# Attention with QK norm, then a mixture of experts: gathers for experts 1 to 4 in a row, and the last expert's second layer with its 16 last tokens first

## The chip, the cores and the metric

The kernel runs on one core of a Trainium2 chip. The metric is the device time of one execution in microseconds (us); lower is better. Three runs of the kernel before took 411.0, 411.21 and 412.35 us, so its median is 411.21 us.

## What is computed

The reference has two parts. The first is attention over 8 batches of 12 heads of 448 tokens with 64 numbers each, with queries and keys normalised (root mean square). The second is a mixture of experts on the 3,584 rows of 768 numbers that this gives: a gate chooses one of 8 experts for each row, each expert keeps the 80 rows with the largest gate weights, and the rest of the output is zero.

```
logits = x @ w_gate
expert_idx = np.argmax(logits, axis=1)
...
out = np.zeros((N, D), dtype=np.float32)
for e in range(E):
    ...
    if len(tok_idx) > capacity:
        gw = gate_w[tok_idx]
        keep = np.argpartition(-gw, capacity)[:capacity]
        tok_idx = tok_idx[keep]
    h = np.maximum(x[tok_idx] @ w1[e], 0.0)
    out[tok_idx] = gate_w[tok_idx, None] * (h @ w2[e])
```

Here E is 8, the capacity 80, w1[e] is 768 x 1024 and w2[e] 1024 x 768.

## The kernel before

The attention takes most of the time. It is followed by a short stage that ends the choice of rows: while earlier batches run, a list of the best 80 rows of each expert is carried along, and after the last batch the lists are made final. The chosen row numbers are written by VectorE into idxG (80 rows by 8 experts, L1115). Attention rows lie in a DRAM tensor, xr_scratch, 780 numbers a row (768 and 12 factors that normalise its heads).

Then comes the expert loop (L1252). Experts are counted from 0 here, as in the code, so "expert 1" is the second one. Expert 0 takes its tokens from matmuls in the stage before. For experts 1 to 7 a gather (L1139), an indirect DMA that GpSimd issues, brings the 80 rows xg into SBUF; VectorE multiplies each by its factors into xn (normal, L1190, three pieces of 256 columns, L1194); TensorE transposes xn (xpose, L1199, pxt, L1209), and a copy puts the result into xgT.

For each expert TensorE does the first layer (ph, L1260: 8 chunks of 128 hidden columns in two halves), and ScalarE takes each half through ReLU into h_sb (L1267). The transposes of the next expert's tokens stand behind the first layer, and behind them the second layer. That has two parts. main (L1239) does the first 64 tokens: 16 matmuls of 384 columns into py, whose upper and lower 64 partitions are the two halves of the output columns. rest (L1245) does the last 16 tokens: 32 matmuls into pz, four quarters on 32 partitions each. rest is done for experts 0 and 7 alone, and for the others in pairs (1 and 2, 3 and 4, 5 and 6) after the second of the pair. VectorE multiplies py by the gate weights into yo (L1284) and pz into yr (L1296), and GpSimd scatters each to the output rows (scatter, L1221, the DMA of L1223).

The order on each engine is the order of the code. GpSimd issues gathers and scatters one after the other on one queue. gather has two ways to hold a transfer back: wait=True puts a memset on VectorE ahead of it, behind=... a copy of one column out of a tile of TensorE's, here the first half of ph of expert 0:

```
            if e == fh == 0:
                gather(2, ph[:CAP, 0, 0:1])
                gather(3)
```

Weights of experts 6 and 7 come late, on SyncE's queue, into the tiles of experts 0 and 1. held (L1229), called behind the first piece of xn of expert 1, starts the first of them; fetch_late (L253) the next two; the last, the second-layer weights of expert 7, are two DMAs of six and two of the eight chunks (L1310), issued after the pair of experts 1 and 2 is done.

Of the kernel before, what the change touches and what calls it, by code (L numbers as in the profile page):

```python
# [10 lines left out]
F32 = mybir.dt.float32  # L11
BF16 = mybir.dt.bfloat16
AF = mybir.ActivationFunctionType
ALU = mybir.AluOpType
# [7 lines left out]
def kernel(  # L22
# [13 lines left out]
    nc = tc.nc  # L36
# [3 lines left out]
    E = moe_w_gate.shape[1]  # L40
    F = moe_w1.shape[2]
    CAP = int(moe_capacity)
# [903 lines left out]
    mpool = mlate[0]  # L946
# [73 lines left out]
    for j in range(NT):  # L1020
        nc.scalar.activation(tied[:, j], row[:, j * 128:(j + 1) * 128], AF.Identity,
                             scale=-1.0, bias=gw[:, j:j + 1])
# [11 lines left out]
    for h in range(4):  # L1034
# [3 lines left out]
                             scale=xo[:, DM + h:DM + h + 1])  # L1038
# [9 lines left out]
    for j in range(NT):  # L1048
# [9 lines left out]
                            op0=ALU.add, op1=ALU.is_lt)  # L1058
# [63 lines left out]
            chosen(1, False)  # L1122
    outs = dram_disjoint_views(out, E + E // 2 + 1)
    xgs = {}
    def gather(e, behind=None, wait=False):

        if e == 1:
            xgs[e] = tpool.tile([128, 1024], F32, tag="beat", name="xg")[:CAP, :XW]
        elif e % 4 == 3:
            xgs[e] = prep.tile([128, NJ + 1, 256], F32, tag="xb", name="xg")[  # L1130
                :CAP].rearrange("p j d -> p (j d)")[:, :XW]
        else:
            xgs[e] = upool.tile([128, 2, S], F32, tag="us", name="xg")[:CAP].rearrange(
                "p u s -> p (u s)")[:, :XW]
        if wait:
            nc.vector.memset(xgs[e][:, 0:1], 0.0)
        if behind is not None:
            nc.vector.tensor_copy(xgs[e][:, 0:1], behind)
        nc.gpsimd.indirect_dma_start(  # L1139
            out=xgs[e], out_offset=None, in_=xr_dram[:, :],  # L1140
            in_offset=bass.IndirectOffsetOnAxis(ap=idxG[:, e:e + 1], axis=0))

    gather(1)
    rows = tpool.tile([CAP, 2, E + 1], F32, tag="move", name="rows")
    nc.vector.tensor_copy(rows[:, 1, :E], psc[:CAP, 1, :E])
    nc.vector.reduce_sum(out=rows[:, 0, :E],
# [21 lines left out]
    def by_two(x, ps):  # L1168
# [7 lines left out]
    gws, gwP = spread[:, :E], spread[:, 2 * E:2 * E + E // 2]  # L1176
    idxM = mpool.tile([128, E], U32, tag="idxM", name="idxM", bufs=1)
    nc.vector.tensor_scalar(idxM[:, :], spread[:, E:2 * E], 2.0, off[:, 0:1],
                            op0=ALU.mult, op1=ALU.add)
# [19 lines left out]
    def xpose(e, xn):  # L1199
        xgT = mpool.tile([128, DC, CAP], BF16, tag="xgT", name="xgT")  # L1200
        pxt = mps.tile([128, DC, CAP], BF16, tag="pxt", name="pxt", bufs=1)
        if e > 1:
            o = [pxt[:, c] for c in range(DC)]
        else:
            first = tpps.tile([128, 2, 1024], BF16, tag="tp", name="pxt")[:, 0, :DC // 2 * CAP]
            o = [first[:, c * CAP:c * CAP + CAP] for c in range(DC // 2)]
            o += [pxt[:, c] for c in range(DC // 2)]
        for c in range(DC):
            nc.tensor.transpose(o[c], xn[:, c * 128:(c + 1) * 128], identb[:CAP, :CAP])  # L1209
        if e > 1:  # L1210
            nc.vector.tensor_copy(xgT[:], pxt[:])  # L1211
        else:
            by_two(xgT, [first, pxt[:, :DC // 2].rearrange("p c t -> p (c t)")])
        xts[e] = xgT

    DN = DM // 2

    def sums(tag, p=128, n=DN):
        return mps.tile([p, n], F32, tag=tag, name="py", bufs=2 if tag == "py" else 1)

    def scatter(k, at, y, h):  # L1221
        o = outs[k] if h == 1 else outs[k].rearrange("n (h d) -> (n h) d", h=h)
        nc.gpsimd.indirect_dma_start(  # L1223
            out=o[:, :], out_offset=bass.IndirectOffsetOnAxis(ap=at, axis=0),
            in_=y, in_offset=None, bounds_check=h * N - 1, oob_is_err=False)
# [13 lines left out]
    def main(e, py, fcs):  # L1239
        for fc in fcs:  # L1240
            for n in range(2):
                product(py[MT * n:MT * n + MT, :], e, fc, slice(0, MT),
                        slice(n * DN, n * DN + DN))
# [8 lines left out]
    for e in range(E):  # L1252
        h_sb = mpool.tile([128, FC, CAP], BF16, tag="hsb", name="h_sb")
        hs[e] = h_sb
        for fh in range(2):
            ph = mps.tile([128, FC // 2, CAP], F32, tag="ph", name="ph")
            for f4 in range(FC // 2):
                fc = fh * (FC // 2) + f4
                for c in range(DC):
                    nc.tensor.matmul(ph[:, f4, :],  # L1260
                                     chunk(e, 0, c)[:, fc * 128:(fc + 1) * 128],
                                     xts[e][:, c, :],
                                     start=(c == 0), stop=(c == DC - 1))
            if e == fh == 0:
                gather(2, ph[:CAP, 0, 0:1])
                gather(3)
            nc.scalar.activation(h_sb[:, fh * (FC // 2):(fh + 1) * (FC // 2), :],  # L1267
                                 ph[:], AF.Relu)
        if e % 2 == 0 and e + 1 < E:
            if e == 0:  # L1270
                xn = normal(1, held)
        if 0 < e < E - 1:
            xpose(e + 1, xn)
        if e < E - 4:
            gather(e + 4, wait=True)
        if 0 < e < E - 2:
            xn = normal(e + 2)
        fcs = range(FC)
        py = sums("py")
        main(e, py, fcs)  # L1280
        if e == 0:
            xpose(1, xn)
        yo = mpool.tile([128, DN], F32, tag="yo", name="yo", bufs=4)
        nc.vector.tensor_scalar(yo[:, :], py[:, :], gws[:, e:e + 1], None, op0=ALU.mult)  # L1284
        scatter(e, idxM[:, e:e + 1], yo[:, :], 2)
        if e % 2 == 0 or e == E - 1:
            k = (e - 1) // 2 if e else E // 2
            g = gwP[:, k:k + 1] if e else spread[:, 3 * E:3 * E + 1]
            single = e in (0, E - 1)
            pair = (e, ) if single else (e - 1, e)  # L1290
            w = len(pair) * DM // 4
            pz = sums("pz")
            rest(pair, pz, fcs)
            yr = mpool.tile([128, DN], F32, tag="yo" if single else "yr", name="yr",
                            bufs=4 if single else 1)
            nc.vector.tensor_scalar(yr[:, :w], pz[:, :w], g, None, op0=ALU.mult)  # L1296
            scatter(E + k, idxP[:, k:k + 1], yr[:, :w], 4 // len(pair))
        if e == 0:
            xn = normal(2)
        if e == 0:  # L1300
            w_tiles[E - 2][1].append(wpool.tile([128, FC, DM], BF16, tag="w2_0", name="w2_sb"))
            fetch_late(E - 2, (1, ))
        elif e == 1:
            w_tiles[E - 1] = ([wpool.tile([128, DC, F], BF16, tag="w1_1", name="w1_sb")], [])
            fetch_late(E - 1, (0, ))
        elif e == 2:
            w2 = wpool.tile([128, FC, DM], BF16, tag="w2_1", name="w2_sb")
            w_tiles[E - 1][1].append(w2)
            for c in (slice(0, FE), slice(FE, FC)):
                nc.sync.dma_start(out=w2[:, c], in_=staged(E - 1, 1)[:, c])  # L1310
# [35 lines left out]
```

## Time and profile before

| What | Value |
|---|---|
| Median of three runs | 411.21 us |
| The profiled execution, its own time | 408.4 us |
| Its span, first to last instruction | 406.6 us |
| TensorE, VectorE, ScalarE, GpSimd busy | 97%, 86%, 79%, 22% of the span |
| Granted TensorE clock | 1.000 |
| DMA, mean over the span | 248 GB/s |

The profiled execution is 2.8 us shorter than the median of the runs. Busy shares are averages over the span, most of which is the attention. The change touches the stretch from the gathers (362.9 us) to the end, so the views below are of that stretch.

### The profile page before, as it was taken

Reading aid. Unit: us, or ns where it says so; the run is one execution under the profiler, and the core shown is the slowest. Engines: PE = TensorE matmul, PEld = TensorE weight load, DVE = VectorE, ACT = ScalarE, POOL = GpSimd, SP = SyncE. Lnnn points to the kernel's source line nnn. Section 1 sums busy time; section 2 is a strip of 40 time slices with the busy share of each in tenths; the row PEclk is TensorE's granted clock in tenths of the full one; section 3 lists DMA queues with packets and bytes.
Section 4 is the critical chain, followed back from the end, with each engine's and each line's share of the span. In section 5 each row is a group of like instructions: output and inputs, shape, how many; then the busy total and the mean of one; then the engine's idle time right before and its main releaser. Section 6 shows DMA issues by size and latency. Waiting matters only on the chain. (4 is left out here: it accounts for less than half of the span.)

```text
span 406.6 us, 12971 instructions
## 1 busy us (share of the span) xinstructions
PE 393.8 (97%) x5447; PEld 191.1 (47%) x5447; DVE 350.6 (86%) x654; ACT 321.2 (79%) x510; POOL 91.3 (22%) x164
## 2 busy tenths in 40 slices
PE   8999999999999999999999999999999999999994
PEld 7334444444444444444444444444444443467673
DVE  5899987998999999997999999979999977883651
ACT  5898979997989879988899789979897878482110
POOL 7300002501032012320251024010520020135533
PEclk9999999999999999999999999999999999999999
DMA  7459999999989899989999999999999359968981
GB/s 254 138 155 202 276 292 261 279 220 302 247 227 261 248 262 253 299 198 233 252 304 220 239 273 232 295 226 280 245 277 271 111 172 378 379 197 234 370 311 58
DMA packets 76315, 100.96 MB, mean 248 GB/s; under 512 B 8568, under 2 KB 65416, under 8 KB 76256
## 3 DMA queue, kind: packets, MB, share of 16 engines
q1 hardware_dynamic: 60192, 70.99, 53.6%
q0 software_dynamic: 16064, 29.13, 39.0%
q8 instruction: 43, 0.70, 0.7%
q14 instruction: 16, 0.13, 0.1%
HBM read 101.11 MB, written 40.28 MB: 348 GB/s over the span
## 5 line engine op out<-in xcount | busy, mean ns | idle before, releaser
L448 ACT ACTIVATE at<-ps 128x896 f32<-128x896 f32 x168 | 146.5, 930 | 4.5 <-PE ps L445 3.3
L445 PE MATMUL ps<-qkT 64*64 64x448 f32 x1344 | 147.3, 548 | 2.4 <-ACT row L646 1.3
L462 PE MATMUL po<-at,vt 64*64 64x448 f32 x1344 | 142.5, 537 | 0.0
L480 DVE TENSOR_TENSOR sm<-sm,at 128x896 f32<-128x896 f32 x120 | 130.7, 1089 | 3.1
L462 PEld LDWEIGHTS po<-at,vt 64*64 64x64 f32 x1344 | 50.1, 133 | 74.0 <-issue 63.6
L445 PEld LDWEIGHTS ps<-qkT 64*64 64x64 f32 x1344 | 43.8, 132 | 66.6 <-issue 26.2
L333 DVE TENSOR_REDUCE ms<-sq 128x14 f32<-128x896 f32 (+1 forms) x50 | 52.1, 1042 | 6.8 <-ACT sq L326 6.7
L363 DVE TENSOR_TENSOR qn<-qk,rs 128x896 f32<-128x896 f32 (+1 forms) x47 | 50.6, 1079 | 1.3
L326 ACT ACTIVATE sq<-qk 128x896 f32<-128x896 f32 (+1 forms) x48 | 44.7, 931 | 2.0 <-DMA qk<-in_q_dram 1.1
L242 POOL COPY mark<-mark 1x1 bf16<-1x1 bf16 x18 | 7.1, 392 | 131.8 <-DVE mark L241 131.8
L765 ACT COPY xb<-xp 128x1024 f32<-128x1024 f32 x24 | 24.3, 1012 | 8.5 <-PE xp L400 7.9
L400 PEld LDWEIGHTS tp<-ident,qn 64*128 64x128 f32 x672 | 23.6, 139 | 12.1 <-issue 5.1
L1267 ACT ACTIVATE h_sb<-ph 128x320 bf16<-128x320 f32 x16 | 7.0, 437 | 26.2 <-PE ph L1260 24.7
L400 PE MATMUL tp<-ident,qn 64*128 64x64 f32 x672 | 27.3, 226 | 0.3 <-DVE qn L363 0.3
L469 ACT COPY us<-po 128x896 f32<-128x896 f32 (+1 forms) x24 | 21.4, 894 | 6.5 <-PE po L462 6.4
L478 DVE TENSOR_TENSOR sm<-at 128x896 f32<-128x896 f32 x24 | 26.0, 1084 | 0.1
L431 ACT COPY qkT<-tp 128x896 f32<-128x896 f32 x24 | 22.0, 917 | 3.4 <-PE tp L400 3.3
L429 ACT ACTIVATE qkT<-tp,gqk 128x896 f32<-128x896 f32 x23 | 23.6, 1025 | 0.0
L497 PE MATMUL zl<-us,wgs 64*32 64x448 f32 x192 | 20.3, 541 | 0.0
L497 PE MATMUL zl<-sm,zsel 64*32 64x448 f32 x192 | 20.1, 541 | 0.0
L400 PEld LDWEIGHTS xp<-ident,us 64*128 64x128 f32 x384 | 14.0, 139 | 12.0 <-ACT at L448 10.6
L1236 PE MATMUL py<-w_sb,h_sb 128*64 128x384 bf16 (+2 forms) x288 | 17.8, 310 | 0.0
(214 smaller groups left out, 425.7 us busy)
## 6 DMA issues: line engine op xcount, KB each, us to landing
vt<-in_v_dram SPq DMA_DIRECT2D x24, 448.0 KB, 6.1
out_dram<-zeros SPq DMA_DIRECT2D x28, 384.0 KB, 8.2
w_sb<-wb_scratch SPq DMA_DIRECT2D x7, 1536.0 KB, 11.4
qk<-in_q_dram SPq DMA_DIRECT2D x23, 448.0 KB, 6.8
qk<-in_k_dram SPq DMA_DIRECT2D x23, 448.0 KB, 6.5
w_sb<-in_moe_w_dram POOLq DMA_DIRECT2D x6, 1536.0 KB, 15.1
xr_scratch<-xb SPq DMA_DIRECT2D x48, 192.0 KB, 7.9
wb_scratch<-in_moe_w_dram POOLq DMA_DIRECT2D x12, 768.0 KB, 10.2
```

What stands on the lines that cost most here:

```text
L326: nc.scalar.activation(o, x, AF.Square)
L333: nc.vector.reduce_sum(out=st[g]["ms"][:, a, lo:hi], in_=st[g]["sq%d" % a][:, lo:hi], axis=AX.X)
L363: e.tensor_mul(qn[:].rearrange("p (x hh) d -> p hh x d", hh=2)[:, h0:h1], qk[:, lo:hi].rearrange("p (hh x) d -> p hh x d", x=NX), rs[:, lo ...
L400: nc.tensor.transpose(o, w, one[p, p], tile_position=(p.start, 0))
L429: nc.scalar.activation(T[:], tp[:, :, :S], AF.Copy, scale=gqk[:, :])
L445: nc.tensor.matmul(ps[u * 64:u * 64 + 64, hh, :S], T1[d, u, x * 64:(x + 1) * 64], T0[d, u, :], start=True, stop=True)
L448: nc.scalar.activation(at[:], ps[:, :, :S], AF.Exp)
L462: nc.tensor.matmul(po[u][hh * D:(hh + 1) * D, u, :S], vt[p, hh * NX + x, :], at[p, hh, :], start=(x == 0), stop=(x == RD - 1))
L478: nc.vector.tensor_add(s["sm"][:], s["at0"][:], s["at1"][:])
L480: nc.vector.tensor_add(s["sm"][:], s["sm"][:], s["at%d" % x][:])
L497: nc.tensor.matmul(t[32 * c:32 * c + 32, r, :S], w, x, start=(i == 0), stop=(i == NQ - 1))
L765: nc.scalar.copy(xb[:].rearrange("p j (u hh d) -> p hh (j u) d", u=2, hh=2), xp[:].rearrange("p hh (k d) -> p hh k d", d=D))
```

## The change

Gathers 1 to 4 (experts 2 to 5 counted from one) are issued in one loop right behind idxG; gather's parameter behind and its copy go, and gather 4 loses its memset. Gathers 5 to 7 stay where they were. In the expert loop the main product and its scatter become a function, most. For experts 0 to 6 it is called where it stood. For expert 7 it is called behind the last tokens' product, and there ScalarE multiplies the left half of py's columns by the gate weights and VectorE the right half.

```diff
-    def gather(e, behind=None, wait=False):
+    def gather(e, wait=False):
...
         if wait:
             nc.vector.memset(xgs[e][:, 0:1], 0.0)
-        if behind is not None:
-            nc.vector.tensor_copy(xgs[e][:, 0:1], behind)
         nc.gpsimd.indirect_dma_start(
             out=xgs[e], out_offset=None, in_=xr_dram[:, :],
             in_offset=bass.IndirectOffsetOnAxis(ap=idxG[:, e:e + 1], axis=0))
 
-    gather(1)
+    for e in range(1, 5):
+        gather(e)
...
-            if e == fh == 0:
-                gather(2, ph[:CAP, 0, 0:1])
-                gather(3)
             nc.scalar.activation(h_sb[:, fh * (FC // 2):(fh + 1) * (FC // 2), :],
                                  ph[:], AF.Relu)
...
-        if e < E - 4:
+        if 0 < e < E - 4:
             gather(e + 4, wait=True)
         if 0 < e < E - 2:
             xn = normal(e + 2)
         fcs = range(FC)
-        py = sums("py")
-        main(e, py, fcs)
-        if e == 0:
-            xpose(1, xn)
-        yo = mpool.tile([128, DN], F32, tag="yo", name="yo", bufs=4)
-        nc.vector.tensor_scalar(yo[:, :], py[:, :], gws[:, e:e + 1], None, op0=ALU.mult)
-        scatter(e, idxM[:, e:e + 1], yo[:, :], 2)
-        if e % 2 == 0 or e == E - 1:
+        last = e == E - 1
+
+        def most():
+            py = sums("py")
+            main(e, py, fcs)
+            if e == 0:
+                xpose(1, xn)
+            yo = mpool.tile([128, DN], F32, tag="yo", name="yo", bufs=4)
+            c = DN // 2 if last else 0
+            if last:
+                nc.scalar.activation(yo[:, :c], py[:, :c], AF.Copy, scale=gws[:, e:e + 1])
+            nc.vector.tensor_scalar(yo[:, c:], py[:, c:], gws[:, e:e + 1], None, op0=ALU.mult)
+            scatter(e, idxM[:, e:e + 1], yo[:, :], 2)
+
+        if not last:
+            most()
+        if e % 2 == 0 or last:
             k = (e - 1) // 2 if e else E // 2
...
             nc.vector.tensor_scalar(yr[:, :w], pz[:, :w], g, None, op0=ALU.mult)
             scatter(E + k, idxP[:, k:k + 1], yr[:, :w], 4 // len(pair))
+        if last:
+            most()
```

On GpSimd the gathers stand in the same place of the queue as before. What each waits for, from the end of the choice of rows to the scatters of expert 0, is before:

```order
L1139 DMA xg<-xr_scratch,idxG 80x780 [waits DMAHW3_49,DMAHW4_49,DMAHW2_49,DMAHW5_49,DMAHW1_49,DMAHW6_49,DMAHW0_49,DMAHW7_49,DMASW1_49,DVE_49]
L1139 DMA xg<-xr_scratch,idxG 80x780 [waits DMASW2_49,DVE_49]
L1139 DMA xg<-xr_scratch,idxG 80x780 [waits DMASW3_49,Activation_49]
L1139 DMA xg<-xr_scratch,idxG 80x780 [waits DMASW4_49,DVE_49]
L1223 DMA out_dram<-yo,idxM 7168x384 [waits DMASW5_49,DVE_49]
L1223 DMA out_dram<-yr,idxP 14336x192 [waits DMASW6_49,DVE_49]
```

and with the change (DVE is VectorE's counter, DMASW and DMAHW are those of earlier transfers):

```order
L1137 DMA xg<-xr_scratch,idxG 80x780 [waits DMAHW3_49,DMAHW4_49,DMAHW2_49,DMAHW5_49,DMAHW1_49,DMAHW6_49,DMAHW0_49,DMAHW7_49,DMASW1_49,DVE_49]
L1137 DMA xg<-xr_scratch,idxG 80x780 [waits DMASW2_49]
L1137 DMA xg<-xr_scratch,idxG 80x780 [waits DMASW3_49,Activation_49]
L1137 DMA xg<-xr_scratch,idxG 80x780 [waits DMASW4_49]
L1222 DMA out_dram<-yo,idxM 7168x384 [waits DMASW5_49,DVE_49]
L1222 DMA out_dram<-yr,idxP 14336x192 [waits DMASW6_49,DVE_49]
```

No row moved; gathers 2 and 4 no longer wait for VectorE.

On VectorE, the last rows of the program (the copy of expert 7's transposed tokens, then the weighing for experts 6 and 7) are before:

```order
L1211 COPY xgT<-pxt 128x480 [waits DVE_49,PE_49]
L1284 TENSOR_SCALAR yo<-py,spread 128x384 [waits DMASW2_49,PE_49]
L1296 TENSOR_SCALAR yr<-py,spread 128x384 [waits DMASW7_49,DVE_49,PE_49]
L1284 TENSOR_SCALAR yo<-py,spread 128x384 [waits DMASW5_49,PE_49]
L1296 TENSOR_SCALAR yr<-py,spread 128x192 [waits DMASW6_49,PE_49]
```

and with the change, where the last two rows are ScalarE's last two (its second half of h_sb of expert 7 and its half of the weighing):

```order
L1210 COPY xgT<-pxt 128x480 [waits DVE_49,PE_49]
L1286 TENSOR_SCALAR yo<-py,spread 128x384 [waits DMASW2_49,PE_49]
L1301 TENSOR_SCALAR yr<-py,spread 128x384 [waits DMASW7_49,DVE_49,PE_49]
L1301 TENSOR_SCALAR yr<-py,spread 128x192 [waits DMASW5_49,PE_49]
L1286 TENSOR_SCALAR yo<-py,spread 128x192 [waits DMASW6_49,Activation_49]
...
L1263 ACTIVATE h_sb<-ph 128x320 [waits PE_49]
L1285 ACTIVATE yo<-py,spread 128x192 [waits DMASW6_49,DVE_49,PE_49]
```

The last tokens' row now comes before the main product's, which is half as wide and waits for ScalarE's row instead of TensorE. On GpSimd the two last scatters change places with them.

## Rows read from the trace of the kernel before

**Rows 1.** Timeline of TensorE, expert loop: start us, us, engine line operation [idle before].

```profile
368.22 0.39 PE L1209 MATMUL pxt<-identb,xn 80*128 80x80 bf16 x6
368.54 0.84 PE L1236 MATMUL py<-w_sb,h_sb 128*32 128x192 bf16 x32
369.32 1.89 PE L1260 MATMUL ph<-xgT,w_sb 128*128 128x80 bf16 x48
371.70 0.91 PE L1209 MATMUL pxt<-identb,xn 80*128 80x80 bf16 x6 [0.49 <-DVE xn L1194]
...
373.97 1.89 PE L1260 MATMUL ph<-xgT,w_sb 128*128 128x80 bf16 x48
...
380.40 1.90 PE L1260 MATMUL ph<-xgT,w_sb 128*128 128x80 bf16 x48
...
383.86 1.90 PE L1260 MATMUL ph<-xgT,w_sb 128*128 128x80 bf16 x48
...
388.74 1.89 PE L1260 MATMUL ph<-xgT,w_sb 128*128 128x80 bf16 x48
...
398.90 2.27 PE L1236 MATMUL py<-w_sb,h_sb 128*64 128x384 bf16 x48
```

**Rows 2.** Timeline of VectorE, the same stretch.

```profile
366.05 0.15 DVE L1138 COPY xg<-ph 80x1 f32<-80x1 f32 x1
366.50 0.83 DVE L1194 TENSOR_TENSOR xn<-xg 80x256 bf16<-80x256 f32 x2 [0.30 <-DMA xg<-xr_scratch,idxG]
...
369.56 0.42 DVE L1296 TENSOR_SCALAR yr<-py,spread 128x192 f32<-128x192 f32 x1
371.22 1.09 DVE L1194 TENSOR_TENSOR xn<-xg 80x256 bf16<-80x256 f32 x3 [1.24 <-DMA xg<-xr_scratch,idxG]
...
376.24 1.09 DVE L1194 TENSOR_TENSOR xn<-xg 80x256 bf16<-80x256 f32 x3 [3.10 <-DMA xg<-xr_scratch,idxG]
...
400.44 0.62 DVE L1284 TENSOR_SCALAR yo<-py,spread 128x384 f32<-128x384 f32 x1 [2.62 <-PE py L1236]
```

**Rows 3.** Timeline of GpSimd: gathers 1 to 3, and the last two scatters.

```profile
362.91 1.07 POOL L1139 DMA_INDIRECT xg<-xr_scratch,idxG  x1 [2.96 <-DMA w_sb<-wb_scratch]
366.47 0.90 POOL L1139 DMA_INDIRECT xg<-xr_scratch,idxG  x1 [2.49 <-DVE xg L1138]
367.68 0.90 POOL L1139 DMA_INDIRECT xg<-xr_scratch,idxG  x1 [0.30 <-ACT h_sb L1267]
...
401.33 0.97 POOL L1223 DMA_INDIRECT out_dram<-yo,idxM  x1 [2.27 <-DVE yo L1284]
402.61 0.97 POOL L1223 DMA_INDIRECT out_dram<-yr,idxP  x1 [0.30 <-issue]
```

**Rows 4.** DMA issues, us to landing: gathers 1 and 3, last two scatters.

```profile
xg<-xr_scratch,idxG POOLq DMA_INDIRECT x1, 3.6
xg<-xr_scratch,idxG POOLq DMA_INDIRECT x1, 8.5
out_dram<-yo,idxM POOLq DMA_INDIRECT x1, 2.6
out_dram<-yr,idxP POOLq DMA_INDIRECT x1, 2.3
```

**Rows 5.** Windows: us, busy by engine, granted clock, DMA share, GB/s.

```profile
363.00:365.00 2.00, 2.00 (x48) 1.47 (x46) 1.56 (x7) 1.26 (x5) 0.98 (x1) 1.00 0.22 41
373.00:375.00 2.00, 2.00 (x43) 1.50 (x40) 0.14 (x2) 0.00 (x0) 0.92 (x1) 1.00 1.03 314
```

**Rows 6.** Timeline of ScalarE: first h_sb of expert 0, last of expert 7.

```profile
366.24 0.44 ACT L1267 ACTIVATE h_sb<-ph 128x320 bf16<-128x320 f32 x1 [1.58 <-DVE xg L1138]
...
399.01 0.44 ACT L1267 ACTIVATE h_sb<-ph 128x320 bf16<-128x320 f32 x1 [0.36 <-PE ph L1260]
```

**Rows 7.** The line that loads expert 7's second-layer weights, and its landings.

```profile
L1310 SPq DMA_DIRECT2D w_sb<-wb_scratch x2: 360/2890/5419, 380.5 to 380.9; - x2
...
DMA to landing us min/median/max: 15.2/15.6/16.1
```

More of the change, by code (lines that the diff above doesn't have):

```diff
@@ L1278 @@
         fcs = range(FC)
-        py = sums("py")
-        main(e, py, fcs)
-        if e == 0:
-            xpose(1, xn)
-        yo = mpool.tile([128, DN], F32, tag="yo", name="yo", bufs=4)
-        nc.vector.tensor_scalar(yo[:, :], py[:, :], gws[:, e:e + 1], None, op0=ALU.mult)
-        scatter(e, idxM[:, e:e + 1], yo[:, :], 2)
-        if e % 2 == 0 or e == E - 1:
+        last = e == E - 1
[13 more added lines that the diff above has]
+        if e % 2 == 0 or last:
             k = (e - 1) // 2 if e else E // 2
             g = gwP[:, k:k + 1] if e else spread[:, 3 * E:3 * E + 1]
-            single = e in (0, E - 1)
+            single = e == 0 or last
             pair = (e, ) if single else (e - 1, e)
@@ L1297 @@
             scatter(E + k, idxP[:, k:k + 1], yr[:, :w], 4 // len(pair))
+        if last:
+            most()
         if e == 0:
             xn = normal(2)
-        if e == 0:
             w_tiles[E - 2][1].append(wpool.tile([128, FC, DM], BF16, tag="w2_0", name="w2_sb"))
```

## The prediction

> **What bounds the kernel now.** I read the views in this order: TensorE's timeline over the expert loop, what VectorE waits for there, when GpSimd issues the gathers and when they land, and last the work behind the final matmul. All before the gathers stays as it was, so only the last 44 us of 406.6 can move.
>
> In the loop TensorE sets the pace. From the start of one first layer (L1260) to the next, odd expert 3 takes 383.86 - 380.40 = 3.46 us, and even expert 4, which also does the last tokens of a pair, 388.74 - 383.86 = 4.88 us [rows 1]. Two experts take longer: expert 1 needs 373.97 - 369.32 = 4.65 us and expert 2 needs 380.40 - 373.97 = 6.43 us [rows 1]. That is 1.19 and 1.55 us too much, 2.74 us together. In both the transposes of the next expert's tokens (pxt) wait for VectorE's xn (for expert 1 the row shows it) [rows 1], and VectorE waited for a gather: 1.24 us before xn of expert 2 at 371.22, and 3.10 us before xn of expert 3 at 376.24 [rows 2]. Behind that are the issue times. Gather 1 is issued at 362.91, gather 2 at 366.47, released by the one-column copy that reads the first matmuls of expert 0, and gather 3 behind it at 367.68 [rows 3]. Gather 1 landed 3.6 us after its issue [rows 4]; gather 2 took about 371.22 - 366.47 = 4.75 us and gather 3 took 8.5 us [rows 4], because the DMA engines filled up meanwhile: their share is 0.22 at 363 to 365 us and 1.03 at 373 to 375 us, in the stretch of the weight loads [rows 5].
>
> The end is a chain: the last matmul, VectorE's weighing, two scatters on GpSimd one behind the other, the landing of the second at 402.61 + 2.3 = 404.91 us [rows 3, 4], and 1.7 us more to the end of the span.
>
> **The change, part by part.**
>
> *Gathers 2, 3 and 4 earlier.* GpSimd's order stays; what goes is the wait of gathers 2 and 4 for VectorE. A gather holds GpSimd for 0.90 to 1.07 us and the next starts 0.30 us later [rows 3], so they start at about 364.28, 365.49 and 366.70; before, GpSimd sat idle for most of that time (2.49 us ahead of gather 2 [rows 3]). It is free at 367.6, and its next scatter needs VectorE's weighing, which begins later (the last tokens' at 369.56 [rows 2]). So their issue costs nothing. Their landing is the unknown. The nearest rows are 3.6 us (gather 1, idle DMA engines) and 8.5 us (gather 3, loaded ones) [rows 4]. I take 4 us for gather 2 and 5 us for gather 3, nearer the first, since both are issued before the first weight load, which goes behind the first piece of xn of expert 1, at about 366.50 + 0.4 [rows 2]: landings at 368.3 and 370.5, at worst 372.8 and 374.0 by these rows. Being issued earlier on the same queue, neither should land later than before, 371.2 and 376.2.
>
> *Expert 1's stall.* From the start of xn of expert 2 to the next first layer went 373.97 - 371.22 = 2.75 us, so an undisturbed 3.46 us asks that xn begins 0.71 us after its own expert's first layer, at 370.03. Behind gather 2's landing VectorE is the next one late: it ends the weighing of expert 0's last tokens at 369.56 + 0.42 = 369.98 [rows 2]. That is just in time. Term: -1.19 us; bounds 0 and -1.19.
>
> *Expert 2's stall.* Likewise 380.40 - 376.24 = 4.16 us, so xn of expert 3 must begin 4.88 - 4.16 = 0.72 us after expert 2's first layer, now at 373.97 - 1.19 = 372.78: by 373.50. Ahead of it VectorE was done 3.10 us before 376.24 [rows 2], at 373.14, now at 371.95. A landing at 370.5 has 3 us to spare; at 374.0 a stall of 0.5 us would stay, and at 376.2 all of both gains would be lost. Term: -1.55 us; bounds +1.19 (nothing gained from both) and -1.55. Gather 4, even 8.5 us after 366.70, lands at 375.2; xn of expert 4 is wanted 0.71 us after expert 3's first layer, at 380.40 - 2.74 + 0.71 = 378.4.
>
> *The copy and a memset go.* The copy takes 0.15 us [rows 2] and ScalarE's first half of h_sb was released by it [rows 6]. I take 0; bounds 0 and -0.15.
>
> *Weights of the last expert.* TensorE asks for them 2.7 us sooner. The last two of the eight pieces of its second-layer weights were issued at 380.9 and landed 16.1 us later, at 397.0 [rows 7]. They were wanted some 1.1 us into the second layer, at 400.0, and are now wanted at 398.90 - 2.74 + 0.86 = 397.0. But three gathers of 80 rows of 3,120 bytes, 0.75 MB, leave the loaded stretch; at its 314 GB/s [rows 5] they took 2.4 us, so this landing should come at about 395. I take 0; bounds 0 and 0.7 us (nothing comes forward, and scatters that are issued earlier push in).
>
> *Last expert: last tokens first.* I count in the times of before, from the start of the second layer at 398.90 [rows 1]. Before: VectorE weighs the main product 1.54 us later, at 400.44 [rows 2], and the second scatter lands at 404.91. After: the first 16 of the 32 small matmuls take 0.39 us (32 took 369.32 - 368.54 = 0.78 [rows 1]), to 399.29. The other 16 need the second half of h_sb, which ScalarE ends at 399.01 + 0.44 = 399.45 [rows 6]; a hand-over between engines takes 0.04 (366.20 to 366.24 [rows 2, 6]) to 0.27 us (VectorE to GpSimd, 401.06 to 401.33 [rows 2, 3]); with 0.12 us, nearer the first, 399.57. The longer main product hid that wait; now 0.28 us of it shows. The small product ends at 399.96, and 1.54 us later, at 401.50, the main product can be weighed. A half on ScalarE has no row: I take 0.44 us, that of 320 columns [rows 6]. VectorE's half takes 0.42 us, as 192 columns do [rows 2].
>
> Do the halves run side by side? The order of the change says no: VectorE's half waits for ScalarE's. The trace has the same pattern: ScalarE's h_sb was released by VectorE's copy out of the same ph tile [rows 6]. So 401.50 + 0.44 + 0.04 + 0.42 = 402.40; undivided it would be 401.50 + 0.62 = 402.12 [rows 2]. With 0.27 us to GpSimd the last scatter is issued at 402.67, where 402.61 was. It is now the larger one, whose like landed after 2.6 us [rows 4]: 405.27. Term: 405.27 - 404.91 = +0.36 us. Bounds: -0.4 (the halves side by side, 0.46 us off, and a landing of 2.3 us) and +0.9 (0.5 us more to GpSimd or in the landing).
>
> The Trainium skill (PSUM — Partial Sum Buffer, section "PSUM bank collisions raise a hardware error") has a rule that speaks against this split: no two engines may access one bank in the same 32 partitions at a time, reads of different columns included. By that rule the halves go in turn and the sum is the one below; without it they could run together and the sum would be 0.46 us lower. The released ScalarE row agrees with the rule.
>
> **Sum.** -1.19 - 1.55 + 0 + 0 + 0.36 = -2.38 us. Against the profiled execution: span 406.6 to 404.2, its own time 408.4 to 406.0. The median of the runs shown, 411.21, lies 2.8 us above that execution; with the same difference, 411.21 - 2.38 = 408.8 us. About 0.3% (1.2 us) is what a measurement of this kernel can tell from no change.
>
> **Rivals.**
>
> *Gather 3 still comes late.* For it: it took 8.5 us when issued 0.8 us after the first weight load, and a landing after 373.5 costs TensorE time. Against: it is now issued 1.4 us before that load, and gather 2, issued 0.4 us before it, took 4.75 us. Between 374.0 and 376.2, so about 375.1, it costs 1.6 us: 410.4 us.
>
> *The weights become the bound.* The last expert's second-layer weights land at 397.0 or later, and the small product asks for all eight pieces within 1 us. Against: the DMA engines have 0.75 MB less to move in that stretch. Price 0.3 to 0.7 us: 409.1 to 409.5 us.
>
> *Gather 1 pays for its followers.* This one ends slower. If the rows of the four gathers are served mixed, gather 1 lands like a loaded one, 8.5 us after its issue instead of 3.6, so 4.9 us later. Xn of expert 1 begins at 366.50 and takes 1.1 us, its transposes run at 368.22 [rows 1, 2], so 0.6 us are free and TensorE stands for 4.3 us; the rest of the sum stays: 408.8 + 4.3 = 413.1 us. The sign turns at a landing 0.6 + 2.38 = 3.0 us later, 6.6 us after the issue. Against it: gather 2 landed some 5 us ahead of gather 3, issued only 1.2 us before it, so they don't land together.
>
> *The halves run side by side after all*: 408.8 - 0.46 = 408.4 us; it is in the forecast's range.
>
> **How the numbers follow.** Forecast (with the side-by-side case) 0.68, own range 408.2 to 409.4. Gather 3 late 0.14. Weights 0.11. Gather 1 late 0.07. Faster by over 0.3% (under 410.0): the forecast less 0.05 for sizes that I have wrong, the weights, and 0.02 of gather 3's case, together 0.76. Slower by over 0.3%: 0.08, gather 1 and a trace of gather 3 with a larger end. Within 0.3%: 0.16. The range of 8 in 10 is 408.0 to 410.3; it leaves out gather 1's case, the far end of gather 3's, and gains over 3.2 us.
>
> **What would show it.** Right: gathers 2 to 4 issued by 367 us; no wait of xn for a gather; experts 1 and 2 at 3.5 and 4.9 us; the last second layer starting 2.7 us earlier; a wait of 0.3 us between its small matmuls; VectorE's 192 columns beginning where ScalarE's end; the last scatter landing after about 2.6 us. Wrong: xn of expert 1 held by its gather past 367.1, TensorE waiting for a weight DMA in the last second layer, or xn of expert 3 waiting more than 1 us.

## The result, and the profile after

The change made the kernel slower: 416.49 us median of 11 runs (413.61 to 417.78) against 411.42 us for the kernel before (11 runs, 410.96 to 413.58). The ratio is 1.010, with a 95% interval of 1.0071 to 1.013, so 2.9 to 5.3 us where the forecast was -2.38 us. The profiled execution took 416.92 us, with a span of 415.2 us; the attention before the changed stretch is as long as it was (the last matmuls on expert 0's own tokens, L1098, start at 363.62 us; 363.98 before).

Timeline of the changed kernel, TensorE (PE), GpSimd (POOL), ScalarE (ACT) and VectorE (DVE), in the columns of [rows 1]:

```profile
363.62 0.38 PE L1098 MATMUL xT<-stayD,xno 80*128 80x80 bf16 x6
365.46 0.91 POOL L1137 DMA_INDIRECT xg<-xr_scratch,idxG  x1 [0.30 <-issue]
365.57 0.36 ACT L1169 CAST xgT<-xT 128x240 bf16<-128x240 f32 x1 [2.04 <-PE hot L1163]
365.62 0.41 DVE L1170 CAST xgT<-xT 128x240 bf16<-128x240 f32 x1 [1.70 <-PE hot L1163]
366.18 1.19 PE L1259 MATMUL ph<-xgT,w_sb 128*128 128x80 bf16 x21 [1.50 <-DVE xgT L1170]
366.67 0.91 POOL L1137 DMA_INDIRECT xg<-xr_scratch,idxG  x1 [0.30 <-issue]
368.47 1.98 PE L1259 MATMUL ph<-xgT,w_sb 128*128 128x80 bf16 x27 [1.10 <-issue]
368.57 0.18 DVE L1174 COPY spread<-hot 128x26 f32<-128x26 f32 x1 [2.54 <-remote]
370.38 2.77 PE L1235 MATMUL py<-w_sb,h_sb 128*64 128x384 bf16 x16
374.71 0.46 PE L1259 MATMUL ph<-xgT,w_sb 128*128 128x80 bf16 x8
...
404.52 1.91 PE L1259 MATMUL ph<-xgT,w_sb 128*128 128x80 bf16 x48
405.60 0.97 POOL L1222 DMA_INDIRECT out_dram<-yr,idxP  x1 [0.52 <-DVE yr L1301]
407.03 0.77 ACT L1263 ACTIVATE h_sb<-ph 128x320 bf16<-128x320 f32 x2 [4.75 <-PE ph L1259]
407.52 2.27 PE L1235 MATMUL py<-w_sb,h_sb 128*32 128x192 bf16 x48 [1.09 <-ACT h_sb L1263]
409.83 0.42 ACT L1285 ACTIVATE yo<-py,spread 128x192 f32<-128x192 f32 x1 [2.03 <-PE py L1235]
410.28 0.42 DVE L1286 TENSOR_SCALAR yo<-py,spread 128x192 f32<-128x192 f32 x1 [1.45 <-ACT yo L1285]
410.98 0.97 POOL L1222 DMA_INDIRECT out_dram<-yo,idxM  x1 [0.90 <-DVE yo L1286]
```

GpSimd does what was forecast: the gathers stand in a row, gather 3 at 365.46 (367.68 before [rows 3]) and gather 4 at 366.67. TensorE doesn't. Its matmuls into xT end at 363.62 + 0.38 = 364.00, but ScalarE's copy of that result starts at 365.57. The first layer of expert 0, in one piece of 1.89 us in the loop of before [rows 1], stands still for 1.10 us in the middle, waiting for nothing that the profile shows ("issue"). VectorE's copy of spread, which reads only a result of TensorE, starts at 368.57, though the last matmuls into that tile (L1163) ended at 364.45 + 0.22 = 364.67. It comes again in the loop: the last first layer starts at 404.52, and ScalarE takes its first half only at 407.03, 2.5 us later, and the second half with it (x2).

Windows of the changed kernel, in the columns of [rows 5]:

```profile
365.00:367.00 2.00, 0.73 (x16) 0.63 (x16) 0.41 (x1) 0.36 (x1) 1.39 (x3) 1.00 0.68 193
367.00:369.00 2.00, 0.87 (x14) 0.76 (x15) 0.39 (x3) 0.11 (x1) 0.58 (x1) 0.63 0.82 211
369.00:371.00 2.00, 2.00 (x26) 1.62 (x25) 1.22 (x8) 0.76 (x2) 0.00 (x0) 0.50 0.19 63
```

TensorE was busy for 1.60 of the 4 us from 365 to 369, and its granted clock then fell to 0.50, the lower of its two levels (1.2 of 2.4 GHz). The second layer's 16 matmuls took 2.77 us there; at a granted clock of 1.00 they take 1.49 us (group 3, below).

### The profile page after: what moved, and what is told of

It is laid out like the page before. It is cut to its first block, busy times and chain, and to the rows that moved or that the text cites. A ratio compares the mean times of both kernels' runs of the same rounds, so it can differ in the third digit from the quotient of the medians.

```text
span 415.2 us, 12970 instructions
## 1 busy us (share of the span) xinstructions
PE 397.1 (96%) x5447; PEld 192.3 (46%) x5447; DVE 350.3 (84%) x652; ACT 320.9 (77%) x511; POOL 91.6 (22%) x164
## 4 chain that ended last, share of the span: by engine, by line
PE 68%; DVE 11%; ACT 7%; issue 7%; POOL 4%; another core or an unknown queue 1%; POOLq 0%; DVEq 0%
PE ps L445 26%; PE po L462 25%; PE zl L497 5%; PE tp L400 3%; DVE sm L480 3%; PE xp L400 3%; POOL out_dram L1222 2%; DVE ms L333 2%; DVE qn L363 2%; ACT at L448 1%; ACT qkT L431 1%; PE mp L688 1%; PE mp L400 1%; ACT zsb L507 1%
## 5 line engine op out<-in xcount | busy, mean ns | idle before, releaser
L1235 PE MATMUL py<-w_sb,h_sb 128*64 128x384 bf16 (+2 forms) x288 | 19.8, 329 | 2.1 <-ACT h_sb L1263 1.6
L1259 PE MATMUL ph<-xgT,w_sb 128*128 128x80 bf16 x384 | 17.1, 207 | 4.0 <-issue 2.3
```

## The experiments

The runs came in six groups, each on a chip of its own and each beside runs of the kernel before on that chip. That turned out to matter, so each group is told with its time of before.

**Which part?** Group 1, before at 408.3 us. Theory A: the row of gathers does it. Theory B: the new end does it. Theory C: it is that gathers 2 and 4 no longer wait for a computing engine. 

The row of gathers alone, against before:

```diff
-    gather(1)
+    for e in range(1, 5):
+        gather(e)
...
-            if e == fh == 0:
-                gather(2, ph[:CAP, 0, 0:1])
-                gather(3)
...
-        if e < E - 4:
+        if 0 < e < E - 4:
```

> The change without its part at the last expert: gathers 1 to 4 in a row, the end as before. Theory A (the run of gathers does the harm: in the changed kernel results of TensorE reach ScalarE and VectorE 0.5 to 2.8 us late in the expert loop, from 364 us on, whenever GpSimd issues a gather or scatter): 416 us, with first halves of h_sb starting 2.5 us or more behind the start of ph where 1.1 is usual, and a granted clock of half speed from about 367 to 374 us. Theory B (the end does it, or the waits are gone and the loss sits in the last expert): 408.6 us, no late results.

The end alone is the change with the gathers as in the kernel before (the lines above taken back):

> The change without its gathers: only the last expert's second layer is as in the change. Theory A: 411.4 + 0.4 = 411.8 us, TensorE's results on time up to the last expert, and the late ScalarE of the last expert gone: small product waits 0.3 us for the second half of h_sb. Theory B: 414 to 417 us.

The order alone is that with the last main product weighed by VectorE alone (the diff stands with group 2):

> Gathers as before; last tokens first in the last expert, but VectorE weighs the whole main product. By the prediction's sum the undivided weighing saves 0.28 us of the 0.36: 411.5 us. If the halves ran side by side they would save, and this would be 0.2 us or more slower than the run with the end of the change.

The whole change with a memset ahead of gathers 2 to 4, against the change:

```diff
     for e in range(1, 5):
-        gather(e)
+        gather(e, wait=e > 1)
```

> The change, with a memset of one column on VectorE ahead of gathers 2 to 4, as gathers 5 to 7 have: they still run in a row, but wait for VectorE. Theory A: as the change, 416 us. Theory C (it is the missing wait for a computing engine, not the row, that makes TensorE's results late): about 409 us and no late results.

Measured: gathers only 0.9936 (0.9915 to 0.9957), end only 1.0017 (0.9997 to 1.0038), order only 1.0019 (1.0000 to 1.0038), memset 0.9957 (0.9932 to 0.9983). No part lost anything like 1%, and the row of gathers gained what was forecast for it. A and B fall as causes that always act, and C is left without a case, since gathers without a memset are fast here too.

**The change itself again.** Group 2, before at 411.7 us.

> The change as it is, unaltered, on the chip of the other runs. Theory D (the late arrival of TensorE's results was a state of that execution or that chip, not a property of the change): the parts behave as in the two single-part runs, so about -2.7 us from the gathers and 0 to +0.7 from the end: ratio 0.993 to 0.997, expert 1 takes 3.5 us from first layer to first layer and expert 2 4.9 us, h_sb starts within 1.2 us of its first layer's start. Theory E (the two parts together do it, with gathers 2 to 4 unheld): ratio 1.007 to 1.013 as before, TensorE's granted clock falls to 0.5 to 0.7 between 367 and 375 us, and h_sb's first half starts 2.4 to 2.9 us behind its first layer in several experts.

And the change with an undivided weighing, against the change:

```diff
-            c = DN // 2 if last else 0
-            if last:
-                nc.scalar.activation(yo[:, :c], py[:, :c], AF.Copy, scale=gws[:, e:e + 1])
-            nc.vector.tensor_scalar(yo[:, c:], py[:, c:], gws[:, e:e + 1], None, op0=ALU.mult)
+            nc.vector.tensor_scalar(yo[:, :], py[:, :], gws[:, e:e + 1], None, op0=ALU.mult)
```

> The change with the last main product weighed by VectorE alone (the gathers in a row and the last tokens first stay). Theory D: fast like all others, ratio 0.993 to 0.997, and the end 0.28 us shorter than in the unaltered change by my sum (402.40 against 402.12). Theory E in the form that the division on ScalarE is the needed partner of the gathers: fast here (0.993 to 0.997) while the unaltered change is slow (1.007 to 1.013). Theory E in the form that the order of the end is the partner: slow here too, 1.007 or more.

Measured: 1.0105 (1.0076 to 1.0135) and 1.0107 (1.0061 to 1.0153). The loss is there again and the divided weighing is not its partner. But group 1 stood beside a before that was 3 us shorter, and so did the profile of before that the prediction was read from (408.4 us). So the next group compared all of them on one chip.

**The program or the chip?** Group 3, before at 408.2 us.

> The kernel before, unaltered, profiled on the chip of this group of runs. Up to now the group in which the parts were fast ran beside a before of 408.3 us, and the groups in which the change was slow beside a before of 411.4 to 411.7 us. Theory F (the chip decides: on some chips TensorE's results reach the other engines late while gathers run): if before takes about 411.5 us here, its trace has the late results too, in the loop's scatters or behind gather 1, and is 2 to 4 us longer than the profile shown (406.6 us); if it takes about 408.3 us, its trace looks like the one shown. Theory G (the exact program decides): its trace looks like the one shown either way. Ratio 0.997 to 1.003.

> The change, unaltered, beside the others of this group. Theory F: beside a before of about 411.5 us a ratio of 1.008 to 1.013 as seen twice; beside one of about 408.3 us a ratio of 0.993 to 0.997, with a span near 404.5 us. Theory G: 1.008 to 1.013 beside either.

> Before with gathers 1 to 4 in a row, its end as before (0.9936 in the earlier group). Theory F: beside a before of about 411.5 us it is slow like the change, 1.007 to 1.013; beside one of 408.3 us 0.993 again. Theory G: 0.991 to 0.996 beside either.

> The change with a memset on VectorE ahead of each of gathers 2 to 4 (0.9957 in the earlier group). Theory F: slow like the change beside a before of about 411.5 us, 1.006 to 1.013, since a memset of one column changes the issue times by a few tenths of a us only; 0.996 beside one of 408.3 us. Theory G: 0.993 to 0.998 beside either.

Measured: before against itself 1.0016 (0.9997 to 1.0036), the unaltered change **0.9951** (0.9934 to 0.9967), gathers only 0.9937 (0.9921 to 0.9954), memset 0.9982 (0.9965 to 0.9999). The same program that lost 1.0% twice gains 0.5% here. Theory G falls; the chip (or something that lasts for a whole group) decides. Timeline of the change in this group:

```profile
365.07 1.89 PE L1259 MATMUL ph<-xgT,w_sb 128*128 128x80 bf16 x48
365.66 0.91 POOL L1137 DMA_INDIRECT xg<-xr_scratch,idxG  x1 [0.30 <-issue]
366.14 0.44 ACT L1263 ACTIVATE h_sb<-ph 128x320 bf16<-128x320 f32 x1 [1.40 <-PE ph L1259]
366.89 1.49 PE L1235 MATMUL py<-w_sb,h_sb 128*64 128x384 bf16 x16
...
369.41 1.90 PE L1259 MATMUL ph<-xgT,w_sb 128*128 128x80 bf16 x48
...
372.87 1.90 PE L1259 MATMUL ph<-xgT,w_sb 128*128 128x80 bf16 x48
...
377.75 1.89 PE L1259 MATMUL ph<-xgT,w_sb 128*128 128x80 bf16 x48
...
396.30 2.61 PE L1235 MATMUL py<-w_sb,h_sb 128*32 128x192 bf16 x48
```

This is the forecast: expert 1 takes 3.46 us, expert 2 takes 4.88 us, and the last second layer starts at 396.30 where before has it at 398.90 [rows 1]. ScalarE takes expert 0's first half 1.07 us after its first layer started, in the middle of gather 3's row.

**What differs on the other chips?** Group 4, before at 411.1 us.

> The kernel before, unaltered, once more with a profile. The last group showed that the change is faster (0.995) beside a before of 408.2 us, on one chip, after 1.010 beside befores of 411.4 and 411.7 us on others. If this chip's before takes about 411.5 us: theory F1 (TensorE's results come late on such a chip whenever GpSimd issues an indirect DMA) expects that this trace has late results too, behind the scatters and gathers of the loop, about 3 us of TensorE's time in all; theory F2 (such a chip is slower everywhere by a little) expects the loop as in the profile shown and the 3 us spread over the attention. If it takes about 408.3 us, its trace is as shown, and nothing is told apart.

> Before with gathers 1 to 4 in a row, its end as before. Beside a before of about 411.5 us: theory F1 expects most of the change's loss, 1.005 to 1.012, with first-layer matmuls of expert 0 interrupted and the granted clock at 0.5 behind them; theory F2 expects the gain of the other chips, 0.993 to 0.996. Beside a before of about 408.3 us: 0.993 to 0.994 by either.

Measured: before against itself 0.9999 (0.9974 to 1.0024), gathers only **1.0085** (1.0049 to 1.0122), where groups 1 and 3 had 0.994. Theory F1 stands and F2 falls: the profile of before itself is another one here. Its last expert, in group 3 (before at 408.2 us):

```profile
395.99 1.89 PE L1260 MATMUL ph<-xgT,w_sb 128*128 128x80 bf16 x48
397.00 0.97 POOL L1223 DMA_INDIRECT out_dram<-yr,idxP  x1 [0.46 <-DVE yr L1296]
397.12 0.44 ACT L1267 ACTIVATE h_sb<-ph 128x320 bf16<-128x320 f32 x1 [3.64 <-PE ph L1260]
397.81 2.27 PE L1236 MATMUL py<-w_sb,h_sb 128*64 128x384 bf16 x48
```

and in group 4, the same program:

```profile
399.12 1.97 PE L1260 MATMUL ph<-xgT,w_sb 128*128 128x80 bf16 x48
400.22 0.97 POOL L1223 DMA_INDIRECT out_dram<-yr,idxP  x1 [0.54 <-DVE yr L1296]
401.68 0.77 ACT L1267 ACTIVATE h_sb<-ph 128x320 bf16<-128x320 f32 x2 [4.80 <-PE ph L1260]
402.17 2.27 PE L1236 MATMUL py<-w_sb,h_sb 128*64 128x384 bf16 x48 [1.08 <-ACT h_sb L1267]
```

In group 3 ScalarE takes the first half 1.13 us after the first layer started, while GpSimd issues a scatter. In group 4 it starts 2.56 us after, and 0.49 us after that scatter's row ends (400.22 + 0.97 = 401.19). All eight profiles of groups 2, 4, 5 and of the result show this at this place (0.46 to 0.54 us behind the scatter's row). In the result's profile the first halves of experts 1, 2, 3 and 7 start 0.43, 0.54, 0.48 and 0.46 us behind the row of an indirect DMA, and 2.91, 2.61, 2.61 and 2.51 us behind their first layer's start: these four keep to the DMA's end. So on these chips results of TensorE that fall due while GpSimd issues an indirect DMA come late, often about 0.5 us behind its row. The rows give no sharper rule: in the same profile expert 5's first half, 2.45 us behind its first layer's start, begins at 397.32, still inside the second of two scatters' rows (396.43 to 397.40), and expert 6's, at 400.56, isn't late (1.14 us) though a scatter's row began 0.11 us before it. It is not every hand-over either: in the changed kernel VectorE's xgT ends at 365.62 + 0.41 = 366.03 and TensorE goes on with it at 366.18, in the middle of a gather (365.46 to 366.37).

Gathers only in group 4, the first layer of expert 0:

```profile
366.12 1.11 PE L1261 MATMUL ph<-xgT,w_sb 128*128 128x80 bf16 x19 [0.91 <-DVE xgT L1172]
367.70 0.34 PE L1261 MATMUL ph<-xgT,w_sb 128*128 128x80 bf16 x5 [0.47 <-issue]
368.43 0.20 PE L1261 MATMUL ph<-xgT,w_sb 128*128 128x80 bf16 x1 [0.39 <-issue]
369.13 1.00 PE L1261 MATMUL ph<-xgT,w_sb 128*128 128x80 bf16 x23 [0.51 <-issue]
370.06 1.49 PE L1237 MATMUL py<-w_sb,h_sb 128*64 128x384 bf16 x16
```

It is cut into four pieces (two in the result's profile), and the last piece starts 1.0 us after the last gather's row ends (367.21 + 0.90 = 368.11). This profile is of one of the group's three shortest executions (412.55 us; the median is 415.51): it shows the hold, but not the lower clock that seven of the ten executions have (last section).

**What of the gathers?** Group 5, before at 412.5 us: H1, the issuing of an indirect DMA on GpSimd; H2, its transfers; H3, any busy GpSimd.

Three fills, and three loads, each against before (room takes the tile of an expert's gather early):

```diff
     gather(1)
+    for e in (2, 3, 4):
+        room(e)
+        nc.gpsimd.memset(xgs[e], 0.0)
```

> Before, with three fills of 80 x 780 numbers on GpSimd (no DMA) between gather 1 and gather 2; about 0.7 to 1 us each. Theory H1 (issuing an indirect DMA on GpSimd holds TensorE's signals back on chips whose before takes about 411.5 us): 0.998 to 1.003, first layer of expert 0 as long as before, 1.9 us. Theory H3 (any busy GpSimd does it): the first layer of expert 0 takes 3 us or more and is interrupted, ratio 1.004 or more on such a chip. On a chip with a before of about 408.3 us both expect 0.998 to 1.003.

```diff
     gather(1)
+    for e in (2, 3, 4, 5, 7):
+        room(e)
+    for e in (4, 5, 7):
+        nc.vector.memset(xgs[e][:, 0:1], 0.0)
+        nc.sync.dma_start(out=xgs[e], in_=xr_dram[:CAP, :])
```

> Before, with three plain DMAs of 80 x 780 numbers from the same DRAM tensor on SyncE's queue, issued at about 364 us behind three one-column memsets on VectorE, into tiles that are used later. Theory H2 (the transfers of the gathers, their packets, hold TensorE's signals back): on a chip whose before takes about 411.5 us the first layer of expert 0 is late or interrupted, by 2 us or more, ratio 1.004 or more. Theory H1 (the issuing on GpSimd does it): the first layer of expert 0 as before, 0.999 to 1.004, the upper end if the loads push gather 1's landing back. On a chip with a before of about 408.3 us: 0.999 to 1.004 by both.

Gathers 1 to 3 in a row, against gathers only:

```diff
-    for e in range(1, 5):
+    for e in range(1, 4):
...
-        if 0 < e < E - 4:
+        if e < E - 4:
```

> Before, with gathers 1 to 3 in a row and gather 4 where it was, behind its memset. Theory H1: on a chip whose before takes about 411.5 us the hold of TensorE in the first layer of expert 0 ends one gather (1.2 us) sooner than with four in a row, so the ratio lies 0.002 to 0.004 under the 1.0085 of four, at 1.004 to 1.007; on a chip with a before of about 408.3 us 0.993 to 0.995, since the gains come from gathers 2 and 3 alone.

Three fills: 1.0068 (1.0046 to 1.0089), above what H1 expected, but not by H3's mechanism. Its timeline:

```profile
363.89 0.38 PE L1098 MATMUL xT<-stayD,xno 80*128 80x80 bf16 x6
363.91 2.15 POOL L1150 MEMSET xg<- 80x780 f32 x3
363.96 2.13 DVE L1155 COPY rows<-rows 80x2 f32<-80x2 f32 x1
364.41 0.36 ACT L1177 CAST xgT<-xT 128x240 bf16<-128x240 f32 x1 [0.60 <-PE xT L1098]
366.37 1.89 PE L1267 MATMUL ph<-xgT,w_sb 128*128 128x80 bf16 x48
```

TensorE's xT, done at 364.27, reaches ScalarE at 364.41 in the middle of the fills, and the first layer is in one piece. What the fills held up was VectorE: a copy that took 0.27 us in the changed kernel took 2.13 us, and expert 0's first layer started 2.48 us after L1098's matmuls, 1.2 us later than in group 4's before (1.27 us). The Trainium skill (Trainium Architecture — The Big Picture, section "What this means for kernel authors") says that VectorE and GpSimd share one pair of ports, as an exclusive lock; this row agrees. H3 falls for TensorE.

Three loads: 1.0033 (1.0012 to 1.0054), inside H1's range. The DMA engines were loaded (share 0.93 from 365 to 367 us), the first layer was in one piece, and ScalarE took its first half 1.32 us after its start. Timeline:

```profile
364.09 1.28 SPq L1152 DMA_DIRECT2D xg<-xr_scratch  x3
365.41 1.88 PE L1269 MATMUL ph<-xgT,w_sb 128*128 128x80 bf16 x48 [0.16 <-DVE xgT L1180]
366.73 0.44 ACT L1276 ACTIVATE h_sb<-ph 128x320 bf16<-128x320 f32 x1 [1.56 <-DVE xg L1142]
368.38 0.77 DVE L1203 TENSOR_TENSOR xn<-xg 80x256 bf16<-80x256 f32 x2 [1.68 <-DMA xg<-xr_scratch,idxG]
```

What they cost is gather 1's landing (xn waits 1.68 us). H2 falls for plain loads; the gathers' own transfers, on GpSimd's queue, weren't tested apart from their issuing.

Gathers 1 to 3 in a row: 1.0031 (1.0008 to 1.0053), under the 1.0085 of gathers 1 to 4 in group 4 and a little under what was expected. Timeline:

```profile
365.86 0.91 POOL L1139 DMA_INDIRECT xg<-xr_scratch,idxG  x1 [0.30 <-ACT xgT L1171]
366.56 2.18 PE L1261 MATMUL ph<-xgT,w_sb 128*128 128x80 bf16 x48 [1.50 <-DVE xgT L1172]
367.92 0.44 ACT L1265 ACTIVATE h_sb<-ph 128x320 bf16<-128x320 f32 x1 [2.28 <-PE ph L1261]
368.67 1.49 PE L1237 MATMUL py<-w_sb,h_sb 128*64 128x384 bf16 x16
```

From the start of L1098's matmuls to expert 0's second layer it takes 368.67 - 364.00 = 4.67 us, with one more gather 5.91 us (group 4), before 3.08 us (group 4). The last gather of the row costs 1.24 us, and from one gather's issue to the next is 1.21 us. This is the size per issued gather that H1 wants; the three of group 4 cost (5.91 - 3.08) / 3 = 0.94 us each on average.

**The end alone again.** Group 6, before at 408.0 us, so this was again a chip of group 1's kind.

> The end of the change alone once more (last tokens first, halves on two engines), gathers as before. Beside a before of about 411.5 us: theory H1 (an indirect DMA that GpSimd issues holds TensorE's results back) expects that the last expert's first half of h_sb comes late in both orders, since the last pair's scatter is issued in both while TensorE is in that first layer, so that the small product's extra wait of 0.28 us vanishes in a wait of about 1 us that is there already: 0.999 to 1.002. If the end were the cause of the change's loss there, it would be 1.004 or more. Beside a before of about 408.3 us: 1.001 to 1.003, as measured.

Measured: 1.0019 (0.9988 to 1.005), as in group 1. On a chip of the other kind the end was not timed alone; there the whole change lost 1.0100 and 1.0105, the row of gathers alone 1.0085, with intervals that overlap.

**The stretches side by side**, from the profiled executions: A from L1098's matmuls to expert 0's second layer, C from there to expert 1's first layer, L from there to the last second layer, each start to start.

| Kernel, before of its group | A us | C us | L us | own time us |
|---|---|---|---|---|
| before, 408.2 | 2.81 | 2.52 | 29.16 | 407.24 |
| change, 408.2 | 2.82 | 2.52 | 26.89 | 406.04 |
| gathers only, 408.2 | 2.82 | 2.52 | 27.27 | 405.69 |
| before, 411.1 | 3.08 | 4.35 | 30.42 | 411.69 |
| gathers only, 411.1 | 5.91 | 2.52 | 30.53 | 412.55 |
| change, 411.4 (the result) | 6.76 | 4.33 | 32.81 | 416.92 |
| change, 411.7 | 6.50 | 3.52 | 32.52 | 416.46 |

On the chips of the second kind (before at 411 us and more) the kernel before pays in C, where its gathers meet the transposes and last tokens of expert 0 (4.35 against 2.52 us). The change moves that hold into A, where each gather after the first stands in the way of expert 0's tokens and first layer, and it is longer there: 6.76 - 3.08 = 3.7 us. By estimate some 0.8 us of that is the lower clock: the 27 matmuls from 368.47 took 1.98 us, where 23 took 1.00 us in group 4 at a granted clock of 1.00. C should then be 2.52, as it is for gathers only, but in the change the lower clock gives it back (16 matmuls in 2.77 instead of 1.49 us are most of it). In L the stalls on gathers are gone, but scatters and later gathers now meet hand-overs: 32.81 us, where the change takes 26.89 us in group 3. From group 4's before to the result's profile the span grows by 415.2 - 409.9 = 5.3 us: A +3.7, C 0, L +2.4, and -0.7 us ahead of A, on two chips of the second kind.

## Why the prediction was wrong

**The issue of gathers 2 to 4: "their issue costs nothing" (the step that failed).** It was costed as GpSimd's time alone. On chips like the one of the result each gather after the first adds 0.9 to 1.2 us to A (group 4, and group 4 against group 5), for four results of TensorE are due between 363 and 368 us: xT, spread and the two halves of h_sb. Measured: A +3.7 us where the prediction had 0, some 0.8 us of it the lower clock that followed; the same clock took away the 1.8 us that C gains. The Trainium skill (Trainium Architecture — The Big Picture, section "What this means for kernel authors") calls the engines independent processors that don't block one another unless a semaphore stands between them. On the chips of groups 1, 3 and 6 the rows agree (ScalarE takes h_sb in the middle of a gather, 366.14 in group 3); on the others the measurement decides, and it differs: the copies of xT and of spread read nothing of a gather, and the same program hands them over on time in group 3.

**The gap between profile and runs (why it couldn't be seen).** The prediction noted that the profiled execution lay 2.8 us under the median and carried it over: "with the same difference, 411.21 - 2.38 = 408.8 us". That difference wasn't a constant. The profile was of a kernel whose hand-overs worked as in groups 1, 3 and 6 (before at 408 us): its ScalarE took the last expert's first half on time, 1.13 us after the first layer started and inside a scatter's row:

```profile
397.08 1.90 PE L1260 MATMUL ph<-xgT,w_sb 128*128 128x80 bf16 x48
398.10 0.97 POOL L1223 DMA_INDIRECT out_dram<-yr,idxP  x1 [0.46 <-DVE yr L1296]
398.21 0.44 ACT L1267 ACTIVATE h_sb<-ph 128x320 bf16<-128x320 f32 x1 [3.64 <-PE ph L1260]
```

The runs shown were, by their times, like those of groups 2, 4 and 5 (none of the 11 is under 410.96 us), in which GpSimd's indirect DMAs hold TensorE's results back. Group 4's profile of before shows the gap as C (+1.8 us) and L (+1.3 us against group 3).

**Expert 1's and expert 2's stalls (-1.19 and -1.55 us).** Right where the chip allows it: 3.46 and 4.88 us in group 3, and no xn waits for a gather behind expert 1's. L got 2.3 us shorter there, all that before's two stalls came to in that group. On the other chips the waits for gathers go too, but later waits take their place, and L got 2.4 us longer than before (32.81 against 30.42).

**The copy and the memset (0).** Right as far as shown: A is 2.82 us without the copy and 2.81 us with it in group 3.

**The weights (0, up to 0.7 us).** Partly the rival: in group 3, gathers only waits 0.33 us for them and the memset kernel 0.77 and 0.21 us; the change itself doesn't. Gathers only, the last second layer:

```profile
396.26 2.27 PE L1237 MATMUL py<-w_sb,h_sb 128*64 128x384 bf16 x48 [0.33 <-DMA w_sb<-wb_scratch]
```

**The end (+0.36 us).** Right in its steps. In group 6 the small and the main product take 2.53 us together, 0.26 us over the 2.27 of [rows 1] (0.28 expected). The last scatter is issued 402.44 - 398.72 = 3.72 us after the second layer starts (402.61 - 398.90 = 3.71 before; 3.77 expected), and the span ends 4.3 us later where 4.0 us was usual. The halves go in turn: ScalarE's ends at 409.83 + 0.42 = 410.25 and VectorE's starts at 410.28, as the prediction's sum has it; the program makes VectorE's half wait for ScalarE's row, so no run shows what the chip would do without that wait. Measured alone: 1.0017 to 1.0019, that is 0.7 to 0.8 us, with intervals from below 0 to 2 us.

**The sum.** Where indirect DMAs don't hold TensorE: -2.38 forecast, 0.9951 or -2.0 us measured (-1.3 to -2.7). Where they do: +5.1 us by the medians, +2.9 to +5.3 us by the ratio's interval.

**The rivals.** Gather 1 paying for its followers (413.1 us) came nearest in time and sign. Its sign in the profile is there too: xn of expert 1 begins at 369.31, after 367.1. But the row ahead of it shows another cause, VectorE's copy of spread at 368.57, which reads a result of TensorE. No rival had GpSimd's issuing hold TensorE, and none had TensorE's clock fall.

## What to carry to other kernels

When the profiled execution and the median of the runs differ by more than the gain that is forecast (2.8 against 2.4 us here), ask for a profile of an execution like those runs before reading any wait from it (group 4's profile of gathers only, 3 us under its median, misses the lower clock in the same way). A change that moves GpSimd's indirect DMAs is to be placed by what TensorE hands over at that time, not only by what the gather is needed for, and timed on more than one chip. On chips like those of groups 1 and 3 the best version of those run is the row of gathers with the old end (0.9937 beside the change's 0.9951 in the same group; their intervals overlap); on the others none of them beat the kernel before.

## What the runs showed that was not expected

- Six chips fell into two kinds: before at 408.0 to 408.3 us on three, at 411.1 to 412.5 us on the other three. Of the 4.4 us between the spans of before in groups 3 and 4 (405.5 and 409.9 us), 3.4 us lie in A, C and L (34.5 and 37.9 us together). What makes the chips differ isn't shown, nor whether one chip stays of its kind.
- On the second kind many of TensorE's results that fall due during GpSimd's indirect DMA come about 0.5 us or more behind its row, and TensorE also stops between matmuls ("issue" waits of up to 1.1 us). Fills on GpSimd and plain loads on another queue don't do this. Which step of the issuing does it stays open.
- TensorE's granted clock fell to 0.50 behind the hold in the changed kernel, but stayed at 1.00 in the profiled execution of gathers only (group 4), where TensorE was busy for 1.75 of the 4 us from 365 to 369:

```profile
365.00:367.00 2.00, 0.98 (x34) 0.82 (x34) 0.41 (x1) 0.21 (x1) 1.60 (x2) 1.00 0.75 178
367.00:369.00 2.00, 0.77 (x8) 0.36 (x7) 0.00 (x0) 0.00 (x0) 0.90 (x1) 1.00 0.69 203
```

The 11 runs of the change fall into two bunches by their mean granted clock: 413.6 to 414.0 us at 0.993 and more (four), 415.3 to 417.8 us at 0.992 and less (seven). So some 2 to 3 us in seven of the eleven runs go with the lower clock; that is not a strict rule, for in group 2 a run of 416.46 us stood at 0.995. Gathers only in group 4 does the same: 412.1 to 412.9 us at 0.996 and more (three), 414.4 to 417.5 us at 0.995 and less (seven), while before stands at 0.995 and less in 3 of its 29 runs there. By the means of these bunches, about half of the change's loss and two thirds of that of gathers only go with the lower clock (estimates). No run separates it from the hold.
- Why L is 2 us longer for the change than for gathers only, though both have the same gathers and scatters in it until the last expert, isn't settled: they ran on different chips.
